# Stacked q and k rows for the heads by queries: written by VectorE copies into their own partitions in place of one DMA per head

## The chip, the cores and the metric

The kernel runs on one core of a Trainium2 chip. The metric is the device time of one execution in microseconds. The kernel before takes 727.61 us (median of three runs, 727.54 to 728.0). Profiles are of one execution each; the one shown for the kernel before took 730.91 us.

## The reference: attention within hash buckets, then a gated MLP

Four batches, 8 heads, 768 positions, head dimension 64. Each q and k row gets a 6-bit bucket from the signs of its products with `proj`; a query sees only the keys of its own bucket. The heads' outputs are joined and go through an MLP whose gate mixes positions.

```python
q_bits = (np.einsum('bhsd,dk->bhsk', q, proj) > 0); k_bits = (np.einsum('bhsd,dk->bhsk', k, proj) > 0)
mask = q_bucket[:, :, :, None] == k_bucket[:, :, None, :]
scores = np.where(mask, scale * np.matmul(q, k.transpose(0, 1, 3, 2)), -1000000000.0)
attn = softmax(scores); attn_out = np.matmul(attn, v)
h = np.maximum(x @ w_in, 0.0); u, v = h[..., :512], h[..., 512:]
v_n = (v - mu) / np.sqrt(var + 1e-06)
v_s = np.einsum('ts,bsd->btd', w_spatial, v_n) + b_spatial[None, :, None]
out = (u * v_s) @ w_out
```

## The kernel before

Heads are numbered n = 0 to 31, eight per batch, and come in pairs p = n // 2 whose q and k lie on 128 partitions, 64 for the even head (e = 0) and 64 for the odd one (e = 1). float32 precision is kept by splitting each operand into a high and a low f16 part and multiplying three times.

Per pair, `load_qk` loads k and q from HBM into `qk`. `hash_rows` forms the bucket signs on PE (L174) and turns them into f16 rows `sg` on DVE (L179, L181). `split_qk` makes `hl`, four planes of 768 columns: 0 is q low, 1 is k high, 2 is q high, 3 is k low. Planes 1 and 2 come from ACT (L187), 0 and 3 from DVE (L188, L189). `hl` has one buffer, so L187 of the next pair waits until all readers of the last are done.

Per head, `build` (L192) puts together a tile `ab` of 128 partitions and four planes (four buffers, taken in turn) from which the scores are multiplied: two matmuls per half row, one over planes 0 and 1 with all 128 partitions (L293), one over planes 3 and 2 with 127 (L294). Planes 0 and 1 hold q low and k high in the lower 64 partitions, q high and k low in the upper 64 (the two cross products in one matmul). Planes 2 and 3 hold k high and q high in the lower 64, and above them the sign rows, 12 partitions from 64 on, whose product of large constants lifts the equal buckets; the rest is constant from the memsets of L86 and L87. The rows are written by DMAs: four small ones for the signs (L200, 9 KB each), L210, which copies the 64 rows of three planes of `hl` as four planes into the lower half (384 KB written, with plane 1 taken twice), and L211, which copies two planes to the upper half (192 KB). Head 0 uses L198 and L204 instead of L210.

Heads 1 to 7 (`KEYS`) work key by key, with a row maximum found beforehand and put into partition 127 of plane 3 by a small DMA (L255). Head 0 and heads 8 to 31 work by queries. For each of six tiles of 128 queries: the scores' matmuls (L293, L294), a copy with row maximum on DVE (L295), the exponential on ACT (L297), the high part on ACT (L300), the low part on DVE or, for tile 0 and 3 (heads below 16) or tile 2 (heads from 16 on), on POOL (L301), and a DMA transpose of both parts (`pt<-pp`, L303, on SP's queue). Five tiles later `weighted` multiplies `pt` with v (L316 to L318). `normalize` and a transposing DMA (L348) hand the result to the MLP of the batch, whose 28 units per batch (L365, L406, L421, L436) are mixed into the heads of the next batch. The last batch's MLP runs after the last head.

The order: a loop over g (six per head) traces the steps with priorities, and the planner of the framework (`schedule_with_timeline_sim`) writes each engine's order from its own durations; the engines then run their lists in order. `build(n + 2)` is traced at tile 0 of head n, and its DMAs on SP stand behind the transpose of that tile (`issue_after`). `split_qk` is traced at tile 3 of an odd head, three tiles before the next build that reads it. SP's queue takes nearly all DMAs: transposes, L210, L211, the loads and the stores. The sign DMAs of heads from 8 on are on ACT's queue.

Of the kernel before, what the change touches and what calls it, by code (L numbers as in the profile page):

```python
# [19 lines left out]
P = 128  # L20
D = 64
NB = 6
# [14 lines left out]
def lsh_attention_spatial_gating(  # L37
# [11 lines left out]
    nc = tc.nc  # L49
    B, NPAIR, _, _, S = kq.shape  # L50
    NH = 2 * NPAIR
    NT = S // P
    HS = S // 2
# [25 lines left out]


    NAB = 4
    NR = D + 2 * NB
    ab = [const.tile([P, 4, S], F16, name=f"ab{i}") for i in range(NAB)]
    for i, t in enumerate(ab):
        eng = nc.vector if i % 2 else nc.gpsimd
# [106 lines left out]
    def build(n):  # L192
        p, e = divmod(n, 2)
        hl, sg, t = st["hl", p], st["sg", p], ab[n % NAB]
        r = slice(D * e, D * e + D)
        q_s, q_h = (BQ_S[n >= NH], BQ_H[n >= NH])
        if n < 1:
            nc.sync.dma_start(out=t[0:D, 2:4], in_=hl[r, 1:3])  # L198
        for j in range(4):
            q_s.dma_start(  # L200
                out=t[D:NR, 3 - j // 2, (j % 2) * HS:(j % 2 + 1) * HS],
                in_=sg[32 * j + 16 * e:32 * j + 16 * e + 2 * NB, :])
        if n < 1:
            q_h.dma_start(out=t[0:D, 0:2], in_=hl[r, 0:2])  # L204
        else:

            top = hl[r, 0:2]
            (ps, pn), (ss, sn), (es, en) = top.ap
            src = replace(top, ap=[(ps, pn), (ss, 2), (ss, 2), (es, en)])
            q_h.dma_start(out=t[0:D].rearrange("p (a b) s -> p a b s", b=2), in_=src)  # L210
        q_h.dma_start(out=t[D:P, 0:2], in_=hl[r, 2:4])  # L211

    def split_v(p):
        if not has_queries(p):
# [42 lines left out]
    def scores_k(n, i):  # L257
        t = ab[n % NAB]
        ps = ps_sc.tile([P, 2, 512], F32, tag="sc", name=f"sp{n}_{i}")[:, :, :HS]
        ks = slice(i * P, (i + 1) * P)  # L260
        for c in range(2):
            cs = slice(c * HS, (c + 1) * HS)
            nc.tensor.matmul(ps[:, c], lhsT=t[:, 1, ks], rhs=t[:, 0, cs], start=True, stop=False)
            nc.tensor.matmul(ps[:, c], lhsT=t[:, 2, ks], rhs=t[:, 3, cs], start=False, stop=True)  # L264
        ex = wk.tile([P, S], F32, tag="pt", bufs=PTB, name=f"ex{n}_{i}")
        st["ex", n, i] = nc.scalar.activation(ex.rearrange("p (c q) -> p c q", c=2), ps, AF.Exp, scale=ISQ).ins  # L266
        st["pt", n, i] = ex
# [11 lines left out]
    def scores(n, i):  # L279
        if n in KEYS:  # L280
            scores_k(n, i)
            return
        t = ab[n % NAB]
        if i == 0:
            st["nb", n] = wk.tile([P, NT], F32, tag="nb", bufs=3, name=f"nb{n}")
            st["mx", n] = wk.tile([P, NT], F32, tag="mx", bufs=4, name=f"mx{n}")
        mx, nb = st["mx", n][:, i:i + 1], st["nb", n][:, i:i + 1]
        ex = wk.tile([P, 2, HS], F32, tag="ex", bufs=EB, name=f"ex{n}_{i}")
        qs = slice(i * P, (i + 1) * P)
        ps = ps_sc.tile([P, 2, 512], F32, tag="sc", name=f"sp{n}_{i}")[:, :, :HS]  # L290
        for c in range(2):
            cs = slice(c * HS, (c + 1) * HS)
            nc.tensor.matmul(ps[:, c], lhsT=t[:, 0, qs], rhs=t[:, 1, cs], start=True, stop=False)  # L293
            nc.tensor.matmul(ps[:, c], lhsT=t[0:P - 1, 3, qs], rhs=t[0:P - 1, 2, cs], start=False, stop=True)  # L294
        nc.vector.tensor_scalar(ex, ps, -float(2 ** 28), None, op0=ALU.max, op1=ALU.max, accum_out=mx)  # L295
        nc.scalar.activation(nb, mx, AF.Copy, scale=-ISQ)
        st["ex", n, i] = nc.scalar.activation(ex, ex, AF.Exp, bias=nb, scale=ISQ).ins  # L297
        at(NT * n + i + G_H, 50)
        pp = wk.tile([P, 2, 2, HS], F16, tag="pp", bufs=PB, name=f"pp{n}_{i}")
        nc.scalar.copy(pp[:, 0], ex)  # L300
        (nc.gpsimd if i in (PL_POOL if n >= 2 * NH else PL_POOL1) else nc.vector).tensor_tensor(out=pp[:, 1], in0=ex, in1=pp[:, 0], op=ALU.subtract)  # L301
        pt = st["pt", n, i] = wk.tile([P, 2 * NT, P], F16, tag="pt", bufs=PTB, name=f"pt{n}_{i}")
        st["tr"] = nc.sync.dma_start_transpose(out=pt, in_=pp.rearrange("p g c k -> p (g c k)")).ins  # L303
# [185 lines left out]
    def at(g, k):  # L489
        tc.cur_priority = int(1000 * (g + 40) + k)  # L490
# [4 lines left out]
    hash_rows(0)  # L495
    split_qk(0)
    build(0)
    load_qk(1)
    build(1)
    load_v(0)  # L500
    at(-1, 0)
# [6 lines left out]
    for g in range(N * NT + LAG):  # L508
        n, i = divmod(g, NT)
        if n < N:  # L510
            at(g + G_S, 0)
            scores(n, i)
            r = n // 2
            at(g + G_P, 300)
# [17 lines left out]
            if i == BI and n + 2 < N:  # L532
                build(n + 2)
# [18 lines left out]
        while wv < N * NT and wv + (LAGK if wv // NT in KEYS else LAG) <= g:  # L552
            m, j = divmod(wv, NT)
# [64 lines left out]
```

## Time and profile before

| | |
|---|---|
| median of three runs | 727.61 us (727.54 to 728.0) |
| the profiled execution | 730.91 us |
| its span, first to last instruction | 729.1 us |
| mean granted TensorE clock | 0.946 |
| DMA packets | 290011, 120.95 MB |
| transposes `pt<-pp` (L303) | 150 |
| `ab<-hl` of 384 KB (L210) and 192 KB | 31 and 34 |

Busy times are those of instructions on an engine; PE is the matmul array, PEld its weight loads, and SPq, ACTq and so on are the engines' queues, which issue DMAs and wait. A row of waits says which instruction waited, for what, the time in all, the count and the longest. The DMA share is the time of all packets over that of 16 engines, and can be over 1, since an engine has more than one packet in flight. Windows are in us from the span's start.

### The profile page before, as it was taken

The numbers are of one execution on the slowest core, as the hardware profiler recorded it, in microseconds if no ns is written. First come the engines' busy times: TensorE is split into PE (matmuls) and PEld (weight loads), VectorE is DVE, ScalarE is ACT, GpSimd is POOL, SyncE is SP. The second block draws the span as 40 slices with busy tenths as digits, with TensorE's granted clock in tenths as the row PEclk, the third lists the DMA queues.
The fourth block names the chain that finished last, engine by engine and source line by source line (L and its number), as shares of the span: only waits on it lengthen the run. The fifth ranks groups of instructions, "written<-read, shape, count | busy, mean of one in ns | idle before, by whom it ended". The sixth has DMA issues, their size and how long they took to land.

```text
span 729.1 us, 14818 instructions
## 1 busy us (share of the span) xinstructions
PE 629.0 (86%) x5735; PEld 392.7 (54%) x5735; DVE 487.4 (67%) x913; ACT 453.2 (62%) x806; POOL 219.8 (30%) x213
## 2 busy tenths in 40 slices
PE   1669798999787976799999898899898888999997
PEld 0237687777344543455555564565455545654553
DVE  4767696534777899956699887678597777735100
ACT  1444474445879868856788777758677778733221
POOL 5201434212234574205103450033132331321503
PEclk9969697999998999999999999899999999999999
DMA  9666554222999999999999999999999999970011
GB/s 237 146 114 177 119 152 119 76 67 71 195 217 227 225 239 195 196 241 211 197 205 200 207 217 202 219 205 203 227 192 174 162 193 205 170 145 1 0 44 45
DMA packets 290011, 120.95 MB, mean 166 GB/s; under 512 B 270740, under 2 KB 273812, under 8 KB 289940
## 3 DMA queue, kind: packets, MB, share of 16 engines
q1 hardware_dynamic: 287636, 119.11, 81.8%
q10 hardware_dynamic: 2304, 0.89, 0.6%
q8 instruction: 45, 0.74, 0.4%
q14 instruction: 26, 0.21, 0.1%
HBM read 28.33 MB, written 6.29 MB: 47 GB/s over the span
## 4 chain that ended last, share of the span: by engine, by line
PE 48%; DMA 26%; DVE 9%; ACT 6%; issue 5%; SPq 4%; POOL 2%; ACTq 1%; DVEq 0%; POOLq 0%
DMA pt<-pp 18%; PE sps L421 7%; PE ops L436 6%; PE ups L406 6%; PE pv L276 6%; PE vps L365 5%; DMA ab<-hl 5%; PE sp L293 3%; PE sp L294 3%; PE pv L316 2%; SPq L303 2%; DVE pp L301 2%; PE pv L318 2%; PE pv L317 2%; DVE ex L295 2%
## 5 line engine op out<-in xcount | busy, mean ns | idle before, releaser
L295 DVE TENSOR_SCALAR_CACHE_REDUCE ex<-sp 128x768 f32<-128x768 f32 x150 | 141.4, 949 | 44.2 <-PE sp L294 42.8
L316 PE MATMUL pv<-vp,pt 128*128 128x65 f16 x900 | 104.9, 197 | 53.2 <-DMA pt<-pp 52.8
L297 ACT ACTIVATE ex<-ex,nb 128x768 f32<-128x768 f32 x150 | 138.3, 931 | 7.5 <-issue 3.3
L300 ACT CAST pp<-ex 128x768 f16<-128x768 f32 x150 | 123.3, 825 | 20.0 <-DMA pt<-pp 13.2
L301 DVE TENSOR_TENSOR pp<-ex,pp 128x768 f16<-128x768 f32 x116 | 119.3, 1032 | 24.2 <-ACT pp L300 23.7
L316 PEld LDWEIGHTS <-pt 128*128 128x128 f16 x900 | 86.0, 101 | 83.6 <-DMA pt<-pp 74.2
L301 POOL TENSOR_TENSOR pp<-ex,pp 128x768 f16<-128x768 f32 x34 | 57.7, 1698 | 209.3 <-ACT pp L300 181.7
L293 PE MATMUL sp<-ab 128*128 128x384 f16 x300 | 103.6, 345 | 17.0 <-DMA ab<-hl 9.7
L317 PE MATMUL pv<-vp,pt 128*128 128x64 f16 x900 | 104.5, 196 | 0.0
L318 PE MATMUL pv<-vp,pt 128*128 128x65 f16 x900 | 104.2, 198 | 0.0
L294 PE MATMUL sp<-ab 127*128 127x384 f16 x300 | 103.8, 346 | 0.4 <-DMA ab<-sg 0.4
L421 PE MATMUL sps<-ws,vn 128*128 128x384 f16 x576 | 101.3, 329 | 0.0
L317 PEld LDWEIGHTS <-pt 128*128 128x128 f16 x900 | 86.5, 100 | 8.2 <-issue 1.7
L318 PEld LDWEIGHTS <-pt 128*128 128x128 f16 x900 | 86.4, 100 | 1.6
L421 PEld LDWEIGHTS <-vn 128*128 128x128 f16 x576 | 55.3, 99 | 35.9 <-issue 2.0
L436 PE MATMUL ops<-wo,g 128*128 128x512 f16 x288 | 70.1, 388 | 1.3 <-ACT o L440 0.9
L276 PEld LDWEIGHTS pv<-vf,ex 128*128 128x128 f32 x504 | 68.6, 209 | 3.8 <-issue 1.6
L365 PE MATMUL vps<-wi,xt 128*128 128x512 f16 x288 | 68.7, 386 | 2.0 <-DMA xt<-xs 2.0
L406 PE MATMUL ups<-xt,wi 128*128 128x384 f16 x384 | 69.5, 334 | 0.0
L276 PE MATMUL pv<-vf,ex 128*128 128x65 f32 x504 | 67.5, 287 | 0.0
L426 POOL TENSOR_TENSOR sy<-sy,u 128x384 f32<-128x384 f32 x32 | 38.5, 1204 | 82.4 <-DVE sy L425 56.7
L266 ACT ACTIVATE ex<-sp 128x768 f32<-128x768 f32 x42 | 33.9, 806 | 38.0 <-PE sp L264 34.4
(88 smaller groups left out, 892.9 us busy)
## 6 DMA issues: line engine op xcount, KB each, us to landing
qk<-kq SPq DMA_DIRECT2D x16, 768.0 KB
ab<-hl SPq DMA_DIRECT2D x31, 384.0 KB
ab<-hl SPq DMA_DIRECT2D x34, 192.0 KB
out<-o SPq DMA_DIRECT2D x24, 256.0 KB
v<-v SPq DMA_DIRECT2D x13, 384.0 KB
raw<-w_in SPq DMA_DIRECT2D x16, 256.0 KB
pt<-pp SPq DMA_TRANSPOSE x150
raw<-w_sp SPq DMA_DIRECT2D x12, 192.0 KB
```

Of the source, the lines that this page charges most:

```text
L276: nc.tensor.matmul(acc[:, qi, :], lhsT=ex[:, qi * P:(qi + 1) * P], rhs=vf[p % 2][:, 2 * i + e, :], start=(i == 0 and qi == 0), stop=(i == ...
L293: nc.tensor.matmul(ps[:, c], lhsT=t[:, 0, qs], rhs=t[:, 1, cs], start=True, stop=False)
L294: nc.tensor.matmul(ps[:, c], lhsT=t[0:P - 1, 3, qs], rhs=t[0:P - 1, 2, cs], start=False, stop=True)
L295: nc.vector.tensor_scalar(ex, ps, -float(2 ** 28), None, op0=ALU.max, op1=ALU.max, accum_out=mx)
L297: st["ex", n, i] = nc.scalar.activation(ex, ex, AF.Exp, bias=nb, scale=ISQ).ins
L300: nc.scalar.copy(pp[:, 0], ex)
L301: (nc.gpsimd if i in (PL_POOL if n >= 2 * NH else PL_POOL1) else nc.vector).tensor_tensor(out=pp[:, 1], in0=ex, in1=pp[:, 0], op=ALU.subtract)
L316: nc.tensor.matmul(acc, lhsT=pt[:, c, :], rhs=vh, start=(i == 0 and c == 0), stop=False)
L317: nc.tensor.matmul(acc[:, 0:D], lhsT=pt[:, c, :], rhs=vl, start=False, stop=False)
L318: nc.tensor.matmul(acc, lhsT=pt[:, NT + c, :], rhs=vh, start=False, stop=(i == NT - 1 and c == NT - 1))
L421: nc.tensor.matmul(ps[:, :HS], lhsT=vn[gv][:, c, d * P:(d + 1) * P], rhs=ws[gw][:, c, hs], start=(k == 0), stop=(k == 3 * NT - 1))
L436: nc.tensor.matmul(ps, lhsT=gt[h][gg][:, c, j * P:(j + 1) * P], rhs=wo[gw][:, c, :], start=(k == 0), stop=(k == 3 * NF - 1))
```

## The change

For the heads from 8 on, L210 is not used. The 64 rows of k and q of a head are kept in the partitions in which they stand in `hl`: the lower 64 for an even head, the upper 64 for an odd one. Two VectorE copies (f16, 64 partitions x 2 planes x 768) write them. The other half gets L211's DMA as before in size, and the sign rows, from partition 64 for even heads and from 0 for odd ones. For odd heads the second score matmul takes all 128 partitions, since partition 127 now holds a row of q and k. The first two odd heads (9 and 11) have the lower half of planes 2 and 3 set to zero on POOL beforehand, in the two buffers that odd heads use.

```diff
-    NR = D + 2 * NB
...
         q_s, q_h = (BQ_S[n >= NH], BQ_H[n >= NH])
+        near = n >= NH
+        z = D - D * e if near else D
+        if near and e and n < NH + NAB:
+            nc.gpsimd.memset(t[0:D, 2:4, :], 0.0)
         if n < 1:
             nc.sync.dma_start(out=t[0:D, 2:4], in_=hl[r, 1:3])
         for j in range(4):
             q_s.dma_start(
-                out=t[D:NR, 3 - j // 2, (j % 2) * HS:(j % 2 + 1) * HS],
+                out=t[z:z + 2 * NB, 3 - j // 2, (j % 2) * HS:(j % 2 + 1) * HS],
                 in_=sg[32 * j + 16 * e:32 * j + 16 * e + 2 * NB, :])
         if n < 1:
             q_h.dma_start(out=t[0:D, 0:2], in_=hl[r, 0:2])
+        elif near:
+            nc.vector.tensor_copy(t[r, 2:4], hl[r, 1:3])
+            nc.vector.tensor_copy(t[r, 0:2], hl[r, 0:2])
         else:
 
             top = hl[r, 0:2]
             (ps, pn), (ss, sn), (es, en) = top.ap
             src = replace(top, ap=[(ps, pn), (ss, 2), (ss, 2), (es, en)])
             q_h.dma_start(out=t[0:D].rearrange("p (a b) s -> p a b s", b=2), in_=src)
-        q_h.dma_start(out=t[D:P, 0:2], in_=hl[r, 2:4])
+        q_h.dma_start(out=t[z:z + D, 0:2], in_=hl[r, 2:4])
...
+        K = P if n % 2 and n >= NH else P - 1
         for c in range(2):
             cs = slice(c * HS, (c + 1) * HS)
             nc.tensor.matmul(ps[:, c], lhsT=t[:, 0, qs], rhs=t[:, 1, cs], start=True, stop=False)
-            nc.tensor.matmul(ps[:, c], lhsT=t[0:P - 1, 3, qs], rhs=t[0:P - 1, 2, cs], start=False, stop=True)
+            nc.tensor.matmul(ps[:, c], lhsT=t[0:K, 3, qs], rhs=t[0:K, 2, cs], start=False, stop=True)
```

## Prediction

> **What bounds the kernel now.** I read the page first, then the engines' busy time by stretch, then the issues of SP's queue and the DMA engines' load around one build, and last who waits for whom.
>
> ```profile
> span 729.1 us, 14818 instructions
> PE 629.0 (86%) x5735; PEld 392.7 (54%) x5735; DVE 487.4 (67%) x913; ACT 453.2 (62%) x806; POOL 219.8 (30%) x213
> DMA  9666554222999999999999999999999999970011
> PE 48%; DMA 26%; DVE 9%; ACT 6%; issue 5%; SPq 4%; POOL 2%; ACTq 1%; DVEq 0%; POOLq 0%
> ```
>
> No engine is busy throughout, but from the eleventh slice on the DMA row shows nothing but nines until the last heads, and transfers are a quarter of the chain that ended last. The second view has the busy time of each engine in six stretches that cover heads 8 to 30; the number after the window is its length, and the last two are the DMA share and GB/s.
>
> ```profile
> core 0: us, PE busy (x) PEld busy (x) DVE busy (x) ACT busy (x) POOL busy (x), PEclk, DMA share, GB/s
> 175.00:250.00 75.00, 62.23 (x604) 36.34 (x603) 57.20 (x111) 63.06 (x120) 29.50 (x25) 0.91 1.03 200
> 250.00:325.00 75.00, 57.59 (x637) 34.70 (x635) 68.00 (x122) 55.60 (x106) 30.00 (x25) 0.95 1.11 217
> 325.00:400.00 75.00, 72.52 (x733) 42.95 (x731) 56.97 (x112) 55.97 (x101) 19.80 (x15) 1.00 1.11 208
> 400.00:475.00 75.00, 64.69 (x698) 40.68 (x696) 57.36 (x100) 55.23 (x93) 20.61 (x15) 0.94 1.11 209
> 475.00:550.00 75.00, 69.49 (x712) 41.16 (x710) 59.74 (x113) 54.32 (x94) 20.89 (x15) 0.97 1.04 207
> 550.00:620.00 70.00, 61.77 (x663) 38.28 (x664) 50.57 (x95) 51.91 (x91) 19.39 (x15) 0.95 1.04 182
> sum 445.00, PE 388.28 PEld 234.10 DVE 349.85 ACT 336.09 POOL 140.18; mean PE 64.71 PEld 39.02 DVE 58.31 ACT 56.01 POOL 23.36
> ```
>
> The DMA share is over 1 in all six (packets overlap on an engine), while PE stands at 57.59 to 72.52 and DVE at 57 to 68 of 75 us. So the DMA engines are the full resource in five of the stretches; in the second one DVE is nearly as full (68.00), and in the third PE is (72.52). After 655 us only the last block's dense layers are left, and nothing that the change touches. Who pays for the full DMA engines: PE, which waits for the transposed weights of the softmax. One row from the waits of each stretch, in their order (us, times, longest):
>
> ```profile
> PE pv L316 <- DMA pt<-pp: 11.1, 7, 3.5
> PE pv L316 <- DMA pt<-pp: 12.5, 10, 2.7
> PE pv L316 <- DMA pt<-pp: 2.4, 5, 0.8
> PE pv L316 <- DMA pt<-pp: 10.3, 7, 3.2
> PE pv L316 <- DMA pt<-pp: 3.1, 3, 1.3
> PE pv L316 <- DMA pt<-pp: 8.5, 8, 2.2
> ```
>
> That is 47.9 us in 40 waits, 1.2 us each.
>
> **What is removed: the DMA of L210, 384 KB per head.** SP's queue around one build, then the load of the DMA engines from 288.5 to 291.25 us, then for contrast in 1 us of transposes and a load that fills 128 partitions, then the issues of two lines (min/median/max in ns):
>
> ```profile
> 286.80 0.97 SPq L210 DMA_DIRECT2D ab<-hl  x1
> 287.83 0.59 SPq L211 DMA_DIRECT2D ab<-hl  x1
> 288.58 2.85 SPq L303 DMA_TRANSPOSE pt<-pp  x1
> ```
>
> ```profile
> DMA packets 202, 0.52 MB, mean 191 GB/s; under 512 B 32, under 2 KB 32, under 8 KB 202
> ```
>
> ```profile
> DMA packets 352, 0.40 MB, mean 397 GB/s; under 512 B 240, under 2 KB 240, under 8 KB 352
> ```
>
> ```profile
> L210 SPq DMA_DIRECT2D ab<-hl x31: 617/717/1474, 9.2 to 598.6; - x31
> L303 SPq DMA_TRANSPOSE pt<-pp x150: 1309/1823/3605, 28.6 to 643.2; - x150
> ```
>
> For 2.75 us the engines move almost only the build's packets (170 of the 202 are over 2 KB), at half the rate of the other stretch, and the transpose issued at 288.58 takes 2.85 us to issue, where the shortest takes 1.31. L210 has two runs of 3072 B on each of 64 partitions, 128 packets, and L211 has 64: at 170 packets in 2.75 us, L210 holds the engines for 128 x 2.75 / 170 = 2.07 us, L211 for 1.04. The second stays. Counted over 175 to 620 us:
>
> ```profile
> ab<-hl SPq DMA_DIRECT2D x22, 384.0 KB
> ```
>
> 22 x 2.07 = 45.5 us of DMA time is the ceiling. The builds of heads 8 and 9 lie ahead of 175 us, where the DMA row has twos, and count for nothing. SP is also freed of the issue itself, 0.72 us x 22 = 16 us of SP's time, in front of the transposes behind it in the same queue. I do not add it: it passes while the DMA engines work off what they have, so it is part of the same gain.
>
> **What is added: 48 copies on DVE**, two per head from head 8, f16, 64 partitions x 1536 elements. The trace has no such copy. Nearest rows (the first as above; the groups with busy us, mean ns):
>
> ```profile
> L181 DVE TENSOR_SCALAR sg<-sg,hc x16: 301/318/1417, 11.1 to 563.3; 128x384 f16<-128x384 f16 x16
> L181 DVE TENSOR_SCALAR sg<-sg,hc 128x384 f16<-128x384 f16 x16 | 9.3, 580 | 0.1
> L179 DVE TENSOR_SCALAR sg<-hp,hc 128x384 f16<-128x384 f32 x16 | 9.8, 611 | 17.5 <-PE hp L174 17.4
> L337 DVE TENSOR_TENSOR x<-pv,rv 128x384 f32<-128x384 f32 x25 | 13.8, 551 | 0.3
> L388 DVE SCALAR_TENSOR_TENSOR rs<-ve,rs 128x3 f32<-128x3 f32 x8 | 1.3, 160 | 0.2
> L301 POOL TENSOR_TENSOR pp<-ex,pp 128x768 f16<-128x768 f32 x34 | 57.7, 1698 | 209.3 <-ACT pp L300 181.7 <-ACT rs L383 14.5 <-ACT nb L296 6.5
> L428 POOL TENSOR_TENSOR g<-sy,g 128x384 f16<-128x384 f32 x32 | 31.6, 988 | 24.5 <-ACT g L427 24.5
> ```
>
> The fixed part is about 155 ns (L388: 3 elements in 160). L337 and L179 show one element per 1.03 ns ((551 - 155) / 384), and some 60 ns more for an operand read per partition (611 - 551), which L181 has too and a copy has not. L181 itself is f16 in and out from SBUF: (318 - 155 - 60) / 384 = 0.27 ns per element. So a copy takes 155 + 1536 x 0.27 = 0.57 us; the other end is the rate of L337, 155 + 1536 x 1.03 = 1.74 us. I take 0.57, since L181 has the copy's types and memory. L181's mean (580) is 0.26 above its median, from a few long ones up to 1417. I add that: 0.83 us, or 1.66 us per head, 48 x 0.83 = 40 us of DVE in all.
>
> A rule speaks against this: the Trainium skill, SBUF — State Buffer, section "Who interferes with whom", says that a copy in DVE's fast two-port modes and any GpSimd instruction exclude one another, each for its whole length. By it a copy would wait only while POOL is busy, 140.18 of 445 us here, for half of an instruction of 1.0 to 1.7 us (L428, L301): an estimate of 0.2 us per copy, 10 us in all against the 12.6 us that I added, which would move the sum below by a third of a us. The long L181s agree with it; nothing here shows what POOL loses in return.
>
> What covers the 40 us: DVE is idle for 445 - 350 = 95 us of the six stretches, and 22 x 1.66 = 36.5 us falls into them. Only in the second is there no room: 68.0 + 4 x 1.66 = 74.6 of 75 us. The copies stand in DVE's order ahead of the next tiles' row maxima (L295) and low parts (L301), for whom PE's slots of scores and SP's transposes wait; so a copy that has to wait holds up both. Its own inputs are old: hl was written three tiles earlier, and the buffer's last reader is two heads back. If that cover failed, each us of waiting would go straight to the transposes.
>
> **What moves at no cost.** The four sign DMAs and L211 keep their sizes and queues and go to the other half of the partitions for odd heads. The second score matmul of odd heads takes 128 rows in place of 127; 128 rows are what L293 has:
>
> ```profile
> L293 PE MATMUL sp<-ab 128*128 128x384 f16 x300 | 103.6, 345 | 17.0 <-DMA ab<-hl 9.7 <-DVE ex L295 6.9 <-DVE mx L244 0.2
> L294 PE MATMUL sp<-ab 127*128 127x384 f16 x300 | 103.8, 346 | 0.4 <-DMA ab<-sg 0.4
> L86 POOL MEMSET ab<- 64x1536 f16 x2 | 2.7, 1374 | 0.1
> ```
>
> Two memsets of 1.37 us (L86's shape) go to POOL for heads 9 and 11, which is 70% idle; uncovered they would cost 2.7 us once. The sign DMAs of those two heads now wait for them in ACT's queue, two heads before anyone reads. Freeing hl for the next pair (L187 waits for its readers) now takes one DMA and two copies in place of two DMAs, all issued three tiles ahead; on the chain that transfer is what ACT waits for, so this is a small help and part of the same DMA time.
>
> **The sum.** In each stretch the gain is the smallest of DMA time taken out (2.07 us per build), PE's wait for transposes, and the room that DVE leaves. With 4, 4, 3, 4, 4 and 3 builds: 175–250 min(8.3, 11.1) = 8.3; 250–325 75 - 74.6 = 0.4; 325–400 min(6.2, 2.4) = 2.4; 400–475 8.3; 475–550 3.1; 550–620 6.2. Together 28.7 us. That takes every us out of the DMA queue as one less of PE waiting. It cannot be so: a build delays the one or two transposes queued right behind it, of six per head, and waits on others stay. I take 0.6 of it, a choice between nothing and all: 17 us. Against the profiled execution (730.9 us, with 1.8 around its span of 729.1) that is 713.9; that execution was 3.3 us above the median of 727.6, and from the median it is 710.6.
>
> **The rivals.**
> *All of it.* The DMA engines alone set the pace and the planner's order lets every freed us count: 28.7 to 45.5 us, 682 to 699 us. For it: DMA shares over 1 everywhere. Against: PE at 72.52 of 75 and DVE at 68 of 75 in the two stretches where there is no room for it.
> *Nothing to speak of.* The transposes come early and PE finds its next limit at once: waits move to the exponentials and to DVE, and the gain is under 5 us: 722 to 729. For it: PE is above 82% in five of six stretches. Against: its idle time there ends on transposes.
> *Slower: DVE becomes the bound.* The mechanism is a copy that stands still as the long L181s did, 1417 - 318 = 1.10 us above the median, or that goes at L337's rate (1.74 us). With the 1.10 a copy costs 1.67 us, 3.3 per head: 350 + 22 x 3.3 = 423 us of DVE in the six stretches. DVE's fullest stretch reaches 68.00 of 75, 0.91; at 0.91 those 423 us need 465, 20 us more than the 445 there are: 748. It decides from 350 + 22 x 2.5 = 405 = 0.91 x 445, that is, from 1.25 us per copy on; just above it the loss is a few us, so 730 to 748. Against: the 16 L181s lie 16 x 0.26 = 4.2 us over their median in all, four such waits. By the Trainium skill's rule named above (SBUF — State Buffer, "Who interferes with whom") it needs POOL to be nearly always in the way, and POOL is busy for a third.
> That the change does not do what it says is excluded: for these heads L210 is not reached. But the planner writes each engine's order anew, and a wait of 1.2 us won or lost in every head would be 26 us; I take zero for it and count it in the width of all cases.
>
> **How the numbers follow.** The forecast, 700 to 722 us, 0.50; all of it (below 700), 0.15; nothing to speak of, 0.19; slower, 0.16. About 0.2% (1.5 us) is what a measurement of this kernel can tell from no change, so the same is 726.1 to 729.1 us. Of the "nothing" case half lies below that (0.10) and half in it (0.09). Faster: 0.50 + 0.15 + 0.10 = 0.75; same 0.09; slower 0.16. The range is 693 to 732: it leaves out the larger part of the "all" case (0.10) and of the slower case (0.10). The likeliest case's own range is 700 to 722.
>
> **What would show it right or wrong.** The group of 384 KB ab<-hl goes from 31 issues to 7; a group of 48 DVE copies appears at 0.57 us median, mean about 0.8; transposes take nearer 1.3 than 1.8 us to issue; PE's wait for pt<-pp in 175–620 us falls from 47.9 to about 30; the DMA share of the stretches falls toward 1. It is wrong if PE's wait for transposes stays while the share falls (they are late for another reason), if the copies' mean is above 1.25 us, or if DVE passes 0.91 in more stretches than the second.

## The result, and the profile after

The kernel after takes 718.62 us (median of four runs, 717.79 to 720.64), the kernel before, run beside it, 727.81 us (727.54 to 731.62). The ratio is 0.9866 with a 95% interval of 0.9827 to 0.9905: faster by 9.2 us, where 17 were forecast. The profiled execution of the kernel after took 718.15 us. Line numbers from 210 on are now 6 to 7 higher, and those of `split_qk` (L187 to L189) one lower: the transposes are L310, the row maximum L302, the low part L308, the matmuls with v L323, and the copies L209 and L210.

First the page: the span, the engines' busy times, the DMA row of the 40 slices and the shares of the chain.

```profile
span 716.4 us, 14854 instructions
PE 618.2 (86%) x5735; PEld 390.3 (54%) x5735; DVE 521.8 (73%) x961; ACT 453.4 (63%) x806; POOL 228.7 (32%) x215
DMA  9666454112989989999999979999989799960011
PE 45%; DMA 22%; DVE 12%; ACT 8%; issue 6%; SPq 4%; POOL 1%; ACTq 1%; DVEq 0%; POOLq 0%
```

The nines of the DMA row now have sevens and eights in between. On the chain the DMAs went from 26% to 22%, and DVE from 9% to 12%. DVE is 34.4 us busier (521.8 against 487.4). The same six stretches as before, in the same columns:

```profile
175.00:250.00 75.00, 61.83 (x640) 37.19 (x638) 65.58 (x120) 63.72 (x123) 33.79 (x26) 0.98 0.93 187
250.00:325.00 75.00, 53.11 (x583) 32.45 (x581) 69.52 (x125) 54.77 (x103) 28.33 (x23) 0.89 0.97 193
325.00:400.00 75.00, 71.51 (x721) 42.79 (x720) 59.52 (x113) 54.43 (x95) 20.22 (x15) 0.98 1.01 185
400.00:475.00 75.00, 69.00 (x765) 43.78 (x762) 65.42 (x119) 58.27 (x104) 22.83 (x16) 1.00 1.02 197
475.00:550.00 75.00, 68.97 (x739) 41.46 (x739) 68.02 (x126) 57.71 (x101) 20.27 (x14) 1.00 0.97 191
550.00:620.00 70.00, 65.30 (x752) 41.99 (x751) 59.97 (x108) 56.09 (x98) 22.19 (x17) 1.00 1.04 185
```

The DMA share was between 1.03 and 1.11 and is now between 0.93 and 1.04, and DVE went up in all six stretches. (The kernel after is further along in the later ones, so a stretch does not hold quite the same work.) How much DMA time went shows in the row of the queue that nearly all transfers use (packets, MB, share of 16 engines' span), in the kernel before and then in the kernel after, with the issues of 384 KB below it:

```profile
q1 hardware_dynamic: 287636, 119.11, 81.8%
```

```profile
q1 hardware_dynamic: 284180, 109.67, 75.8%
ab<-hl SPq DMA_DIRECT2D x7, 384.0 KB
```

0.818 x 729.1 = 596.4 us became 0.758 x 716.4 = 543.0 us: 53.4 us for 24 transfers, 2.2 us each. What was to be removed was removed. Now what was added, the copies (min, median and max in ns; then busy time and mean):

```profile
L209 DVE COPY ab<-hl x24: 541/556/1518, 129.8 to 561.7; 64x1536 f16<-64x1536 f16 x24
```

```profile
L210 DVE COPY ab<-hl 64x1536 f16<-64x1536 f16 x24 | 17.0, 709 | 0.2
L209 DVE COPY ab<-hl 64x1536 f16<-64x1536 f16 x24 | 16.8, 701 | 0.1
```

They take 33.8 us in all, and wait for nothing (0.3 us of idle time before them). Last the waits from 175 to 620 us, of the kernel before and then of the kernel after (us, times, longest):

```profile
PE pv L316 <- DMA pt<-pp: 48.0, 40, 3.5
DVE ex L295 <- PE sp L294: 39.4, 26, 3.7
ACT nb L296 <- DVE ex L295: 20.2, 21, 4.0
ACT hl L187 <- DMA ab<-hl: 10.0, 6, 3.7
```

```profile
PE pv L323 <- DMA pt<-pp: 44.6, 39, 3.6
ACT nb L303 <- DVE ex L302: 35.1, 36, 3.5
DVE ex L302 <- PE sp L301: 24.5, 26, 4.1
ACT hl L186 <- DMA ab<-hl: 12.5, 7, 3.3
```

The reader is to see two things. The DMA engines are relieved, but PE's wait for transposes hardly moved, 48.0 to 44.6 us. And ACT now waits 15 us longer for the row maxima that DVE makes. It looks as if the transposes were late for another reason than before; the experiments are to show it.

### The profile page after: what moved, and what is told of

The parts are those of the page before. It is cut to its first block, busy times and chain, and to the rows that moved or that the text cites. A ratio compares the mean times of both kernels' runs of the same rounds, so it can differ in the third digit from the quotient of the medians.

```text
span 716.4 us, 14854 instructions
## 1 busy us (share of the span) xinstructions
PE 618.2 (86%) x5735; PEld 390.3 (54%) x5735; DVE 521.8 (73%) x961; ACT 453.4 (63%) x806; POOL 228.7 (32%) x215
## 4 chain that ended last, share of the span: by engine, by line
PE 45%; DMA 22%; DVE 12%; ACT 8%; issue 6%; SPq 4%; POOL 1%; ACTq 1%; DVEq 0%; POOLq 0%
DMA pt<-pp 14%; PE sps L428 7%; PE ups L413 6%; PE ops L443 5%; PE vps L372 5%; PE pv L282 5%; DVE pp L308 3%; DMA ab<-hl 2%; PE sp L300 2%; PE sp L301 2%; PE pv L323 2%; SPq L310 2%; DVE ex L302 2%; ACT ex L304 2%; PE pv L325 2%
## 5 line engine op out<-in xcount | busy, mean ns | idle before, releaser
L302 DVE TENSOR_SCALAR_CACHE_REDUCE ex<-sp 128x768 f32<-128x768 f32 x150 | 141.6, 949 | 27.2 <-PE sp L301 26.1
L323 PE MATMUL pv<-vp,pt 128*128 128x65 f16 x900 | 105.0, 196 | 49.8 <-DMA pt<-pp 49.7
L304 ACT ACTIVATE ex<-ex,nb 128x768 f32<-128x768 f32 x150 | 139.8, 932 | 6.6 <-ACT nb L303 2.6
L308 DVE TENSOR_TENSOR pp<-ex,pp 128x768 f16<-128x768 f32 x116 | 123.2, 1064 | 11.4 <-ACT pp L307 10.8
L323 PEld LDWEIGHTS <-pt 128*128 128x128 f16 x900 | 85.3, 100 | 78.9 <-DMA pt<-pp 68.5
L308 POOL TENSOR_TENSOR pp<-ex,pp 128x768 f16<-128x768 f32 x34 | 59.5, 1750 | 204.1 <-ACT pp L307 146.6
L300 PE MATMUL sp<-ab 128*128 128x384 f16 x300 | 101.9, 340 | 18.5 <-DMA ab<-hl 9.2
L301 PE MATMUL sp<-ab 127*128 127x384 f16 (+1 forms) x300 | 102.2, 341 | 0.0
L372 PE MATMUL vps<-wi,xt 128*128 128x512 f16 x288 | 66.7, 379 | 0.8 <-DMA xt<-xs 0.8
L413 PE MATMUL ups<-xt,wi 128*128 128x384 f16 x384 | 67.3, 326 | 0.0
L433 POOL TENSOR_TENSOR sy<-sy,u 128x384 f32<-128x384 f32 x32 | 36.7, 1148 | 76.6 <-DVE sy L432 54.7
L303 ACT ACTIVATE nb<-mx 128x1 f32<-128x1 f32 x150 | 29.5, 196 | 49.0 <-DVE ex L302 48.2
```

What stands on the lines that cost most here:

```text
L301: nc.tensor.matmul(ps[:, c], lhsT=t[0:K, 3, qs], rhs=t[0:K, 2, cs], start=False, stop=True)
L323: nc.tensor.matmul(acc, lhsT=pt[:, c, :], rhs=vh, start=(i == 0 and c == 0), stop=False)
L413: nc.tensor.matmul(ps[:, :HS], lhsT=wi[gw][:, c, d * P:(d + 1) * P], rhs=xt[c][:, gx, hs], start=(k == 0), stop=(k == 3 * NPAIR - 1))
```

## The experiments

**The first theories.** Theory A: the relief of the DMA engines is worth the forecast 17 us or more, and the copies give about half of it back. Theory B: the copies are hidden, as the prediction had it, and the relief is worth only the 9 us that were measured. (The kernels without copies, and the one without the second transfer, leave out part of the scores' inputs, as their expectations say.) Ratios are to the kernel before, run on the same chip in the same batch; 0.001 is 0.73 us.

**No copies, and every copy twice.**

```diff
-            nc.vector.tensor_copy(t[r, 2:4], hl[r, 1:3])
-            nc.vector.tensor_copy(t[r, 0:2], hl[r, 0:2])
+            pass
```

> The kernel after without its 48 DVE copies: the rows of q and k that they write keep what earlier heads left there, so this leaves out part of the scores' inputs; transfers, matmuls and all else stay. Theory A (the relief of the DMA engines is worth about 17 to 20 us and the copies on DVE give half of it back): 705 to 711 us, DVE busy falls by 34 us, PE's wait for pt<-pp in 175 to 620 us well under 44.6 us. Theory B (the copies are hidden; freeing 2 us of DMA time per head is worth no more than what was measured, because the transposes are late for another reason): 715 to 721 us, that is within 3 us of the kernel after's 718.6, and the wait stays near 45 us.

```diff
-            nc.vector.tensor_copy(t[r, 2:4], hl[r, 1:3])
-            nc.vector.tensor_copy(t[r, 0:2], hl[r, 0:2])
+            for _ in range(2):
+                nc.vector.tensor_copy(t[r, 2:4], hl[r, 1:3])
+            for _ in range(2):
+                nc.vector.tensor_copy(t[r, 0:2], hl[r, 0:2])
```

> The kernel after with each of the 48 copies done twice (same bytes, so the result is the same): DVE gets another 34 us. Theory A (DVE's time is on the path for about a third to a half): 729 to 737 us, 10 to 18 us over the kernel after. Theory B (copies hidden): 716 to 723 us.

Without copies 703.7 us, ratio 0.9641 (0.9588 to 0.9694); with twice the copies 749.05 us, ratio 1.026 (1.02 to 1.032). So 48 copies more or fewer are 0.0225 (16 us) on the one side and 0.039 (29 us) on the other: theory B fell. Theory A's ranges were missed too, by 1 us and by 12. In the kernel with twice the copies ACT waits 57.8 us for the row maxima from 175 to 620 us, against 35.1 in the kernel after, and PE's wait for DVE to free the scores, 7.9 us there, becomes a wait of weight:

```profile
ACT nb L303 <- DVE ex L302: 57.8, 34, 5.6
PE sp L300 <- DVE ex L302: 20.1, 15, 2.9
```

**Is there more to be had from the DMA engines?** The other transfer of a build (192 KB) left out, with the copies in place; then a copy and a transfer of 192 KB in place of two copies; then the change for heads 16 to 31 alone.

```diff
-        q_h.dma_start(out=t[z:z + D, 0:2], in_=hl[r, 2:4])
+        if not near:
+            q_h.dma_start(out=t[z:z + D, 0:2], in_=hl[r, 2:4])
```

> The kernel after without the remaining 192 KB DMA of each head from 8 on (the cross-product rows of planes 0 and 1 keep what earlier heads left, so this leaves out part of the scores' inputs): another 1.04 us of DMA time per head is freed, 22 x 1.04 = 23 us, and with it the wait of ACT's L186 for that transfer. Theory A (DMA time is worth about 0.4 of itself): 708 to 713 us. Theory B (the transposes are late for another reason): 715 to 721 us.

```diff
-            nc.vector.tensor_copy(t[r, 0:2], hl[r, 0:2])
+            q_h.dma_start(out=t[r, 0:2], in_=hl[r, 0:2])
```

> The kernel after with only the planes 2 and 3 copied by DVE (24 copies); planes 0 and 1 come by a DMA of 192 KB per head, so half of the DMA time comes back. If both the relief and the cost go by their amount: 24 / 2 - 15 / 2 = 4.5 us of gain, 722 to 725 us. If the first half of the relief is worth more than the second (the kernel after without the other DMA too gained nothing more): 713 to 718 us.

```diff
-        near = n >= NH
+        near = n >= 2 * NH
```

> The change for heads 16 to 31 alone (heads 8 to 15 as in the kernel before). If every head gains the same: 728 - 9.2 x 16 / 24 = 721 to 723 us. If the copies cost most while the weights are being converted on DVE (up to about 290 us, DVE at 66 to 69 of 75), and give nothing there: 716 to 720 us.

Leaving out the second transfer gave 721.5 us, ratio 0.9884 (0.9836 to 0.9933), where theory A had 708 to 713: no better than the kernel after, although PE's wait for transposes fell to 31.3 us. With the copies there, less DMA time alone bought nothing, in an order planned anew. Half the change gave 736.53 us, 1.0111 (1.0056 to 1.0166), slower than before, and the change for half of the heads 729.28 us, 0.9992 (0.9963 to 1.0021). Neither theory has a place for these two: parts of the change don't add up to it. In each of these kernels the planner had written every engine's order anew, which the last experiments take up; that this is the whole of these two misses was not shown.

**Is it the number of copies, their place, or the engine?** Theory C: the price is DVE's time, some 0.44 us per us of copying (the 15 us between the kernels with and without copies, over 34). Theory D: it is the burst, since the copies of both heads of a pair stand together. First one copy of 3072 elements in place of two; then the two held apart, each behind a row maximum of its own; then the copies on GpSimd.

```diff
-            nc.vector.tensor_copy(t[r, 2:4], hl[r, 1:3])
-            nc.vector.tensor_copy(t[r, 0:2], hl[r, 0:2])
+            nc.vector.tensor_copy(t[r].rearrange("p (a b) s -> p a b s", b=2), src)
```

> The kernel after with one copy per head of four planes (k high read twice, 3072 elements) in place of two of 1536: 24 instructions of 155 + 3072 x 0.26 = 0.96 us, at most 7 us less of DVE. Theory C: 3 us less, 714 to 717 us. Theory D: the burst goes from about 2.8 to 2.2 us, 714 to 718 us. It does not tell the two apart; it tells what the fixed part and the waits of 24 instructions are worth.

```diff
-            nc.vector.tensor_copy(t[r, 2:4], hl[r, 1:3])
-            nc.vector.tensor_copy(t[r, 0:2], hl[r, 0:2])
+            with tc.issue_after(st["row"]): nc.vector.tensor_copy(t[r, 2:4], hl[r, 1:3])
+            st["more", n] = lambda: nc.vector.tensor_copy(t[r, 0:2], hl[r, 0:2])
...
+            if i == 2 and ("more", n + 2) in st:
+                with tc.issue_after(st["row"]): st.pop(("more", n + 2))()
```

> The kernel after, with the same 48 copies but held apart in DVE's order: the first copy of a head behind the row maximum of tile 0 of the head two before, the second behind that of tile 2. In the trace of the kernel after, the four copies of a pair stand together, right behind L187 and L188 of that pair. Theory C (what costs is DVE's time, 34 us of it at about 0.44): no change from the kernel after, 716 to 721 us. Theory D (what costs is the burst: some 5 us in which DVE does little for the softmax, scores fill both PSUM slots and PE stops): most of the 15 us that the copies cost comes back, 705 to 711 us.

```diff
-            nc.vector.tensor_copy(t[r, 2:4], hl[r, 1:3])
-            nc.vector.tensor_copy(t[r, 0:2], hl[r, 0:2])
+            nc.gpsimd.tensor_copy(t[r, 2:4], hl[r, 1:3])
+            nc.gpsimd.tensor_copy(t[r, 0:2], hl[r, 0:2])
```

> The kernel after with its 48 copies on GpSimd in place of DVE; POOL is 32% busy. A copy of 64x1536 f16 there at 1.4 to 1.7 us (the POOL memset of that size took 1.37), 67 to 82 us more of POOL. Theory A: DVE is relieved, 706 to 713 us, unless the POOL instructions make DVE's two-input instructions wait as long as the copies took. Theory B: 716 to 722 us.

(`src` is the source of the transfer L216, which takes plane 1 twice.) One copy per head: 718.77 us, 0.9862 (0.981 to 0.9914), as the kernel after; its copies take 29.0 us in place of 33.8, so the number of instructions was not the price, as far as an interval of 4 us to each side can tell. Held apart: 724.42 us, 0.9906 (0.9868 to 0.9945), no better, which speaks against theory D, though with another order. On GpSimd: 770.14 us, 1.055 (1.0492 to 1.0608), the slowest of all, which neither theory had. Its groups, and below them the row of the kernel before for the same low part of k:

```profile
L209 POOL COPY ab<-hl 64x1536 f16<-64x1536 f16 x24 | 46.1, 1920 | 34.9 <-ACT hl L186 30.1 <-PE sp L301 4.2
L210 POOL COPY ab<-hl 64x1536 f16<-64x1536 f16 x24 | 45.3, 1885 | 15.2 <-PE sp L269 6.6 <-issue 5.9 <-DVE hl L187 1.2
L188 DVE SCALAR_TENSOR_TENSOR hl<-qk,hl 128x768 f16<-128x768 f32 x16 | 31.5, 1967 | 0.0
```

```profile
L189 DVE SCALAR_TENSOR_TENSOR hl<-qk,hl 128x768 f16<-128x768 f32 x16 | 17.5, 1095 | 0.0
```

A copy takes 1.9 us on GpSimd against 0.7 on DVE, and the DVE instruction that makes the last plane of `hl`, next to which the copies run, nearly doubles, from 1095 to 1967 ns. It has two inputs in SBUF. Of its 16 instructions in that trace, the two beside no POOL instruction took 0.95 us, and ten of the eleven beside these copies 1.67 to 4.77. The Trainium skill, SBUF — State Buffer, section "Who interferes with whom", says that such a DVE instruction contends with a GpSimd instruction that reads SBUF: the trace agrees.

**The order held fixed.** Everything so far compared kernels whose orders differ too: between the kernel after and the one without copies, 264 of DVE's rows and 1,700 of PE's stand in another place. Theory O: it is that other order, not the copies, that was paid. Each of the last four kernels is held, on every engine, to an order that the planner wrote for another kernel. `made` builds the kernel with or without the copies, with or without a transfer of 384 KB in their place, and in a given order, and returns it with its own order; the loop ties each instruction behind the one ahead of it in that order. The copies and the transfer themselves are left out of the order, so the planner places them.

```diff
-            nc.vector.tensor_copy(t[r, 2:4], hl[r, 1:3])
-            nc.vector.tensor_copy(t[r, 0:2], hl[r, 0:2])
+            for a in tc.copy_planes: tc.extra.append(nc.vector.tensor_copy(t[r, a:a + 2], hl[r, a // 2:a // 2 + 2]).ins.name)
+            if tc.top_dma: tc.extra.append(top_rows(q_h, t[r], hl[r, 0:2]))
...
+    def made(copies, top_dma, order=None):
...
+    nc, _ = made(False, False, made(True, False)[1])
...
+    for ks in order.values():
+        for a, b in zip(ks, ks[1:]):
+            tc.add_manual_dep(traced[b], traced[a].name, how, reason="order")
```

> The kernel after without its 48 copies (the query-side halves of t keep what earlier heads left there, so that part of the scores' inputs is left out), with every other instruction of each engine held in the order that it has in the kernel after. The run without copies before this one was 15 us faster than the kernel after, but its planner had also put 264 rows of DVE and 1,700 of PE in other places. Theory A, the copies' own DVE time is what was paid: 702 to 707 us. Theory O, most of those 15 us came of the planner's other order: 714 to 719 us.

The second has the copies, in the order planned for the kernel without them:

```diff
+    nc, _ = made(True, False, made(False, False)[1])
```

> The kernel after with all its work, its other instructions held in the order planned for the kernel without copies. Nothing is left out. Theory A (the copies' own time): the order alone is worth at most 3 us, 716 to 722 us. Theory O (the order is what was paid): 704 to 711 us.

The third has the transfer of 384 KB in place of the copies, in the order of the kernel after:

```diff
+    nc, _ = made(False, True, made(True, False)[1])
```

> No copies; the whole 128-partition shift of 384 KB is restored, as in the kernel before, and everything else stands in the order of the kernel after. Nothing is left out. It differs from the kernel before by order alone, and from the fixed-order run without copies by the transfers alone. If the relief of the DMA queue gave the change's gain: 725 to 731 us, that is 21 to 26 us above the run without copies if that one comes to 702 to 707. If the new order gave it: 715 to 720 us.

The fourth has the order of the kernel after, with the copies held apart as above:

> The kernel after with all its work and its order, but the copies held apart: the first behind the row maximum of tile 0 of the head two before, the second behind tile 2, so that no four stand together. Theory D (the price is the burst of four ahead of the row maximum): 705 to 711 us. Theory A (the price is the time itself): 716 to 721 us.

The first took 710.26 us, ratio 0.9723 (0.968 to 0.9766); the second 726.32 us, 0.9937 (0.9906 to 0.9967); the third 738.76 us, 1.0115 (1.0074 to 1.0156); the fourth 721.24 us, 0.9856 (0.9796 to 0.9917). The first lies between the two theories' ranges, the second is slower than both had it, and the third is slower than both had it and slower than the kernel before, with the same amount of work in another order. (Its transfers fill, for an odd head, the half of `ab` that the copies fill, where the kernel before fills the other one, and it has the two memsets of the kernel after.) Set out by work and order, all as ratios to the kernel before:

| work | own order | the order of the kernel after | the order planned without copies |
|---|---|---|---|
| 384 KB transfer (before) | 1 | 1.0115 | not run |
| neither | 0.9641 | 0.9723 | 0.9641 |
| copies (after) | 0.9866 | 0.9866 | 0.9937 |

Down a column only the work changes. In the order of the kernel after, the relief of the DMA engines is worth 1.0115 - 0.9723 = 0.0392, 28.5 us by the two medians of one chip, and the copies cost 0.9866 - 0.9723 = 0.0143, 10 us. In the order planned without copies they cost 0.9937 - 0.9641 = 0.0296, 22 us. In the orders planned for each, relief and copies are 0.0359 (26 us) and 0.0225 (16 us). Along a row only the order changes: in all three rows the work runs slower in an order that was planned for other work, by 0.0115, 0.0082 and 0.0071, which is 5 to 8 us. From the two intervals of each, the 10 and the 22 us are uncertain by some 4, and these 5 to 8 us by 3 to 5. No run holds a kernel to its own order, so a price of the holding itself is not excluded; the fourth run, held to the order of the kernel after and with the ratio of that kernel, speaks against one, though its copies stand elsewhere. So theory A holds, since the copies cost time in either order, and theory O has a part, since the order decides how much. Theory D is not confirmed by the fourth run either: its ratio is the kernel after's.

The waits from 175 to 620 us show who pays. The third kernel (the transfer), then the first (neither); the kernel after, in the same order, stands above with 44.6, 35.1 and 12.5 us:

```profile
PE pv L323 <- DMA pt<-pp: 54.8, 39, 4.0
ACT nb L303 <- DVE ex L302: 20.9, 26, 2.0
ACT hl L186 <- DMA ab<-hl: 28.0, 8, 5.7
```

```profile
PE pv L323 <- DMA pt<-pp: 33.6, 33, 3.5
ACT nb L303 <- DVE ex L302: 18.5, 28, 2.0
ACT hl L186 <- DMA ab<-hl: 11.0, 5, 3.3
```

Without the transfer PE's wait for transposes falls by 21.2 us, and ACT's for the readers of the last `hl` by 17.0. With the copies the first rises again by 11.0, and ACT's wait for row maxima by 16.6. These sums do not give the time by themselves: with the copies apart (the fourth kernel) they are 32.7 us for transposes and 27.2 for row maxima (in a profiled run of 715.54 us), and the median time is the kernel after's within the interval. One place in the timeline shows it, DVE in the kernel after:

```profile
410.26 0.95 DVE L188 SCALAR_TENSOR_TENSOR hl<-qk,hl 128x768 f16<-128x768 f32 x1
411.13 1.11 DVE L209 COPY ab<-hl 64x1536 f16<-64x1536 f16 x2
412.27 0.56 DVE L344 TENSOR_TENSOR x<-pv,rv 128x384 f32<-128x384 f32 x1
412.75 1.45 DVE L399 TENSOR_SCALAR vr<-vr,mv,rs 128x512 f32<-128x512 f32 x3
414.11 0.95 DVE L308 TENSOR_TENSOR pp<-ex,pp 128x768 f16<-128x768 f32 x1
414.98 1.98 DVE L210 COPY ab<-hl 64x1536 f16<-64x1536 f16 x2
416.99 0.96 DVE L302 TENSOR_SCALAR_CACHE_REDUCE ex<-sp 128x768 f32<-128x768 f32 x1
```

Who waited for that row maximum, in ACT's timeline of the same kernel:

```profile
417.99 0.20 ACT L303 ACTIVATE nb<-mx 128x1 f32<-128x1 f32 x1 [3.01 <-DVE ex L302]
```

And the same place without the copies, in the same order (the first kernel), DVE and then ACT:

```profile
406.10 0.95 DVE L188 SCALAR_TENSOR_TENSOR hl<-qk,hl 128x768 f16<-128x768 f32 x1
406.96 0.55 DVE L344 TENSOR_TENSOR x<-pv,rv 128x384 f32<-128x384 f32 x1
407.43 1.45 DVE L399 TENSOR_SCALAR vr<-vr,mv,rs 128x512 f32<-128x512 f32 x3
408.80 0.95 DVE L308 TENSOR_TENSOR pp<-ex,pp 128x768 f16<-128x768 f32 x1
409.67 0.95 DVE L302 TENSOR_SCALAR_CACHE_REDUCE ex<-sp 128x768 f32<-128x768 f32 x1
410.66 0.20 ACT L303 ACTIVATE nb<-mx 128x1 f32<-128x1 f32 x1 [0.54 <-DVE ex L302]
```

From the low part of `hl` to the row maximum it is 6.73 us with the four copies (410.26 to 416.99) and 3.57 without (406.10 to 409.67). The difference of 3.16 us is the copies' 1.11 + 1.98 = 3.09 nearly to the whole: DVE had no gap there. ACT waited 3.01 us for that row maximum, against 0.54 without the copies, and by the kernel's order of work the exponential, the low part, the transpose and PE come after it.

No version with the whole computation beat the kernel after: one copy per head and copies held apart are its equals.

## Why the prediction was right, and where its terms were not

**The direction, and the range.** Faster was right, and 718.6 us lies in the likeliest case's 700 to 722. The size was off by 8 us, and two terms that make it up were further off than that, one against the other. The 0.2% that was to be told from no change was too fine: the interval of the ratio reaches 0.4% to each side.

**The transfer's price.** 2.07 us per L210 was forecast, and 2.2 measured (53.4 us for 24). The rate read off one stretch of 2.75 us was good enough.

**The factor of 0.6 was too low.** Of 28.7 us, the sum over the stretches, 17 were taken, on the argument that a build delays only one or two transposes. The relief measured 26 us with each kernel's own order and 28.5 in one order. The 28.7 had given the second stretch next to nothing because of the copies, which these runs don't have; with the 7.0 us that DVE leaves there without them (75 - 68.0) the bounds come to 28.7 - 0.4 + 7.0 = 35.3 us, and what was measured is 0.74 to 0.81 of that. So a cut was in place, but 0.6 was a guess, and too deep. Whether the bound of each single stretch held was not tested.

**"What covers the 40 us" was wrong.** The copies' length was right: 0.556 us in the median against 0.57, 0.705 in the mean against 0.83, 33.8 us in all against 40. The Trainium skill, SBUF — State Buffer, section "Who interferes with whom", says that a DVE instruction in a two-port mode and a GpSimd instruction block each other, the second until the first has finished. From that the prediction had an estimate of 0.2 us per copy, and the means stand 0.15 over the medians; the 11 copies that took over 600 ns all ran beside a POOL instruction, and the 30 beside none took at most 558: this trace agrees. But the copies were put in DVE's idle time, 95 us of 445, as if it could be had anywhere. The text named the place rightly, ahead of the next row maxima and low parts, and then priced only a copy that has to wait. The copies waited for nothing, and their own length went in part on the path: 10 us of their 33.8 in one order, 22 in another, 16 with each kernel in its own. The step that failed is the cover: a share of idle time over a stretch says nothing of the moment.

**"hl was written three tiles earlier" was wrong as well.** In the timeline above the planner put the copies right behind the instruction that writes `hl`, two of the four with nothing between, and all four ahead of the next row maximum. In six of the eleven pairs from 170 us on all four stand so, in the others one or two. By itself that cost little, since holding them apart gained nothing that could be measured.

**"I take zero for it"**, the planner's new order: it is 5 to 8 us where it could be measured, nearly as large as the gain itself. In the order of the kernel after the change is worth 1.0115 - 0.9866 = 0.025, 18 us, and the forecast's 17 would have been near; against the kernel before in an order of its own 9 are left. That 17 is near 18 was luck: 28.5 - 10.4 in place of 17 - 0. Which way the order counts depends on where one starts: the order of the kernel after is 8 us worse for the work of the kernel before, and 5 us better for its own work than the order planned without copies.

**The signs.** The 384 KB group went to 7 issues, the copies to 48, the DMA share toward 1, but the transposes' issue went only from 1823 to 1656 ns in the median, where nearer 1.3 than 1.8 us was forecast:

```profile
L310 SPq DMA_TRANSPOSE pt<-pp x150: 1306/1656/3915, 28.2 to 630.5; - x150
```

PE's wait for transposes was to fall to about 30 us; it did where there were no copies (33.6, or 22.3 in the order planned without them) and stayed at 44.6 with them. That is the mark that the prediction itself set for being wrong, a wait that stays while the share falls, and it pointed at the copies. The small help for ACT's wait for `hl` didn't show between the kernels before and after, 10.0 to 12.5 us; in one order it is not small, 28.0 us with the transfer and 11.0 without. The memsets on POOL and the moved sign DMAs were not tried alone.

**The rivals.** "DVE becomes the bound" named the right engine and the wrong condition: the copies' mean stayed at 0.7 us, under its 1.25, DVE passed 0.91 only in the second stretch (69.52 of 75), and yet DVE took back 0.36 of the gain in one order (10.4 of 28.5 us) and 0.63 with each kernel in its own (16.4 of 26). With 48 more copies the time came to that rival's, 749 us against its 748, but not by its condition: DVE was busy there for 390.0 us of the 445 from 175 to 620 us, 0.88.

## What to carry to other kernels

Work moved to an engine that is two thirds busy is not free: ask which instruction of that engine someone waits for, and whether the new work will stand right ahead of it, and charge its full length there. Over all the copies it came to 0.3 to 0.6 us per us of copying here, by the order. Price the removed and the added term each by a run that does it alone, because a sum that comes near can hide two errors. Where a planner writes the order, a difference of 5 to 8 us in 720 between two versions can be its doing; hold the order fixed before saying which part of a change was worth what, and in more than one order, since a part can be worth 10 us in one and 22 in the other.

## What the runs showed of the hardware that was not expected

- The same f16 copy of 64 x 1536 elements takes 0.556 us on DVE in the median and 1.9 us in the mean on GpSimd, and there a DVE instruction next to it went from 1095 to 1967 ns in the mean.
- PE was busy for 618.2 us after and 629.0 before, with the same 5,735 matmuls: of the 12.7 us of span that went, 10.8 are shorter matmuls and 1.9 less idle time. In the three large groups of the MLP the means went from 334 to 326 ns, 386 to 379 and 388 to 381, while the medians stayed. What went is long ones: one group as an example (min, median and max), before and after, and below it the windows from 400 to 620 us, before and after, where the granted clock (the third number from the end) went from 0.95 to 1.00.

```profile
L365 PE MATMUL vps<-wi,xt x288: 376/379/634, 158.5 to 669.2; 128*128 128x512 f16 x144
L372 PE MATMUL vps<-wi,xt x288: 376/379/390, 158.1 to 656.4; 128*128 128x512 f16 x144
400.00:620.00 220.00, 195.95 (x2071) 120.12 (x2070) 167.67 (x307) 161.46 (x277) 60.88 (x45) 0.95 1.06 200
400.00:620.00 220.00, 203.27 (x2250) 127.23 (x2248) 193.41 (x351) 172.07 (x301) 65.28 (x47) 1.00 1.01 191
```

The clock drops for a few us at a time: from 415.4 to 418.8 us of the kernel before it is 0.50, and the matmuls L294 there take 0.53 us, where their median is 0.326. Over the whole span its mean is nearly the same (0.946 and 0.949), because up to 130 us it is lower in the kernel after (0.82 against 0.86). Why it drops, and whether PE's waits bring it about, was not tested. In the fixed order, too, part of the relief lies here: PE was busy for 627.9 us with the transfer and 615.9 without, in one profile of each.
